# Attention denominators read over 128 partitions, and rows and down products in another order, in an adaLN block with linear attention and a GEGLU FFN

## The chip, the core and the metric

One core of a Trainium2 chip runs the whole block in one launch. The metric is device time in microseconds; three runs of the kernel before gave 782.70, 782.91 and 783.98, a median of 782.91. TensorE (PE) multiplies matrices out of weights loaded beforehand (PEld), VectorE (DVE) and ScalarE (ACT) work on rows, GpSimd (POOL) helps a little, and SyncE (SP) issues the DMAs, which 16 DMA engines carry out.

## What is computed

`x` is [1, 2048, 1024] bf16, with 32 heads of 32, `w_gate` and `w_up` [1024, 3584], `w_down` [3584, 1024], `c` [1, 1024], `w_mod` [1024, 6144]. Cut to what matters:

```
mod = silu(c) @ w_mod                       # six rows of 1024: sa ca ga sb cb gb
h   = layernorm(x) * (1 + ca) + sa
q, k, v = h @ wqkv                          # 32 heads
pq, pk  = phi(q), phi(k)                    # phi(t) = (t + 1 if t > 0 else exp(t)) + 1e-6
kv  = sum_s pk[s] v[s]^T ;  z = sum_s pk[s] # per head
o   = (pq @ kv) / (pq @ z + 1e-6)           # the divisor is "den"
x   = x + ga * (o @ wo)
h   = layernorm(x) * (1 + cb) + sb
out = x + gb * ((gelu(h @ w_gate) * (h @ w_up)) @ w_down)
```

## The kernel before

**Order of the work.** Every instruction is recorded with what it reads and writes; a tracker of intervals makes the waits. TensorE and SP run in the order in which the program records their instructions. The order of DVE, ACT and POOL between two marks (from the k projections to the loads of FFN unit 0) is made by a list scheduler from a table of costs and the due times of what depends on an instruction. All DMAs of the main part go through SP's one queue, in order; they take eight lanes (semaphores) in turn, and a DMA waits until the one before it in its lane is complete. The tokens are 16 chunks of 128, in four superblocks `sg` of four chunks.

**Until about 127 us** TensorE makes k and q (L880, L934), in bf16.

**127 to 191 us**: 24 m_tiles (L895) of 16 matmuls with 341 or 342 columns multiply the transposed pk with x. After each of them a table `HOOK` (L1302) puts in smaller work, by name: `kv<g>` is kv_prod (L913), eight 128-column matmuls on a transposed m_tile that m_t (`mT<g>`, L703, a transposing DMA into `mtb`) has brought; `w<i>` is w2_pair (L1201, copied out at L1208), which folds kv and wo into `W2`; `modp` is mod_pass (L1227), which sums modulation rows over partitions with mod_rows (L840), copies them out (L847), stores 4 rows of 512 f32 to DRAM (L849) and loads them as columns `sbT`, `cbT` (L1230); `gbr` is gb_rows (L809), the same for gb from `HLG`, which gb_hilo (L801; its last DVE subtraction is called mlo7) writes; `den<i>` is the divisor of two superblocks (L1240).

```
HOOK = {0: "ga", 6: "kv0", 10: "kv1", 11: "w0", 13: "kv2", 15: "modp kv3 z32", 16: "den0", 17: "w1 rb0.0 rb0.1", 18: "",
        19: "kv4", 20: "den1 ps0.0", 21: "gbr", 22: "ps0.1", 23: "rb2.0"}
```

**1/den.** den adds 1e-6 (L1245), takes the reciprocal (L1246) and stores 128 rows of 256 f32 in DRAM (L1248) as `scr_rd[sg, h, k, g, t]`: h one of two halves of 256 tokens, k one of four heads within a group, g one of eight groups. In `PQ[sg]`, partition 32k + d holds component d of head k of each group. rb_load (L1260) brings 1/den into `RB`, with each of the four rows k copied to 32 partitions: per half four DMAs, one for each k. pq_scale (L1273) multiplies pq by it on DVE, four instructions of two groups for each half, each after all four DMAs of its half.

**191 to 257 us**: the wo stage (L1283), in chunks c0 to c15 of 16 matmuls with 512 columns; chunk c needs PQ of its half (c0, c1: half 0 of superblock 0, and so on). On DVE x1 (L1291) adds a chunk to x, then come the second layernorm and T2, a transposing DMA (`h2a`, `h2b`). A table `SLOT` (L1769) says what is recorded after each chunk: the other pq_scales, rb3, loads of x, and `wt_dma(0)` (L1371), FFN unit 0's weights, after chunk 4.

**241 to 600 us**: 28 units of the FFN's first half (L1458), each a 2 x 2 block product in seven products (Strassen's scheme in Winograd's form), with sums on DVE and ACT.

**598 to 776.6 us**: the down stage in eight pairs of chunks, again seven products (L1672) of up to 14 matmuls each. P1 and P2 take y and `w_down` in bf16, P5, P6, P7, P3, P4 sums in fp32 (`sb` by L1643 and L1648). d_pair (L1722) runs them in the order 1, 5, 6, 2, 7, 3, 4; P7 goes on in P6's bank; copies (L1692, L1698) and adds (L1695) join the banks, evac (L1576, L1577) scales by gb and adds x. The rows of y for the next pair (`ya`) come back from DRAM by y_in (L1571), x by x_in (L1568). Hooks for each pair (L1885) place these. Pair 0 is mixed with plain products (L1593). The tail is the last evac and its DMA.

Of the kernel before, what the change touches and what calls it, by code (L numbers as in the profile page):

```python
# [330 lines left out]
def bass_adaLN_cond__linear_attn_block__geglu_ffn__prompt_kernel(  # L331
# [18 lines left out]
    with ExitStack() as es:  # L350
# [183 lines left out]
        def r_2k(off, name):  # L534
            return [(off, off + 2048, name)]
# [256 lines left out]
        def gb_acc(j, dc):  # L792
# [4 lines left out]
            else:  # L797
                sch.op(V, lambda e: e.scalar_tensor_tensor(acc[:, :], src, SILF[:, dc:dc + 1], acc[:, :], op0=ALU.mult, op1=ALU.add),
                       rd=rs_ + rng, wr=rng, note=f"macc{6 + j}.{dc}")

        def gb_hilo(j):  # L801
            acc, rng = GA_[j]
            sch.op(A, lambda e: e.activation(HLG[:, j, 0, :], acc[:, :], ACTF.Copy), rd=rng, wr=r_hlg(j, 0), note=f"mhi{6 + j}")
            sch.op(V, lambda e: e.tensor_tensor(HLG[:, j, 1, :], acc[:, :], HLG[:, j, 0, :], ALU.subtract), rd=rng + r_hlg(j, 0), wr=r_hlg(j, 1), note=f"mlo{6 + j}")

        o_gb = [None]

        def gb_rows():
            mod_rows(((0, 2, 5, lambda j, h: (HLG[:, j, h, :], r_hlg(j, h))),))  # L809
            o_gb[0] = mod_store(2, 5, MRG, [(OFF_TMP + 4096, OFF_TMP + 5120, "mrg")], 2)  # L810

# [380 lines left out]
        def z32():  # L1192
            sch.op(V, lambda e: e.tensor_tensor(Z32[:], BM32[:], ZCOLS[:, :].unsqueeze(2).to_broadcast([P, NG, NH]), ALU.mult),
                   rd=r_sm("bm32") + r_sm("zcols"), wr=r_sm("z32"), note="z32")

        def w2_pair(i, b0=4):
            for hf in range(2):
                for r in range(2):
                    for h in range(2):
                        b, g = b0 + 2 * r + hf, 2 * i + h  # L1200
                        sch.op(T, lambda e, b=b, g=g, h=h, r=r, hf=hf: e.matmul(ps_all[64 * h:64 * h + 64, b * 512:(b + 1) * 512], KVT[64 * r:64 * r + 64, g, 0:64],  # L1201
                               WO[64 * r:64 * r + 64, g, hf * 512:(hf + 1) * 512], start=True, stop=True),
                               rd=r_kvt(g, g + 1) + r_wo(g, hf * 512, (hf + 1) * 512), pwr=pr(b), note=f"w2 {i}.{hf}", overwrite_ok=True)
            for r in range(2):
                b, g = b0 + 2 * r, 2 * i + r
                w_, p_ = W2[:, g, :], ps_all[:, b * 512:(b + 2) * 512]
                eng = V if i > 1 and r else A
                sch.op(eng, lambda e, w_=w_, p_=p_, eng=eng: e.activation(w_, p_, ACTF.Copy) if eng == A else e.tensor_copy(w_, p_),  # L1208
                       prd=pr(b) + pr(b + 1), wr=r_w(OFF_WK, "w2", g), note=f"w2cp{g}")
# [15 lines left out]
        def mod_pass():  # L1225
            assert mdone[0] >= 48 and not late
            mod_rows(((2, 4, 5, hl_src),))  # L1227
            o_r = mod_store(4, 5, MROW[1], r_2k(OFF_ROW + 2048, "mrow1"), 1)
            for dst, nt, a0 in ((SBT, "sbT", 0), (CBT, "cbT", 2)):
                sch.dma(Q, lambda e, dst=dst, a0=a0: e.dma_start(dst[:, :], scr_row[1, a0:a0 + 2, :].rearrange("a (b p) -> p (a b)", p=P)),  # L1230
                        wr=r_sm(nt), deps=[o_r], note=nt)

# [19 lines left out]
        o_rd = {}  # L1252
        rb_ops = {}

        def rb_load(sg, hs=(0, 1)):
            i = sg % 2
            for h in hs:
                made = []
                for k in range(HPG):
                    made.append(sch.dma(Q, lambda e, h=h, k=k: e.dma_start(  # L1260
                        RB[i][32 * k:32 * (k + 1), h, :, :].rearrange("p a b -> p (a b)"),
                        scr_rd[sg, h, k:k + 1, :, :].rearrange("k g t -> k (g t)").to_broadcast([32, NG * HW])),
                        wr=r_rb(i, h) if k == 0 else (), deps=made[0].deps if k else [o_rd[sg // 2]], note=f"rb{sg}.{h}.{k}"))
                rb_ops[sg, h] = made

        GH = [((0, 2), (2, 4)), ((4, 6), (6, 8))]

        def pq_scale(sg, h, gs):
            i, t0 = sg % 2, h * HW
            for g0, g1 in gs:  # L1270
                ap = PQ[sg][:, g0:g1, t0:t0 + HW]
                rng = r_pq(sg, g0, g1, t0, t0 + HW)
                sch.op(V, lambda e, ap=ap, i=i, h=h, g0=g0, g1=g1: e.tensor_tensor(ap, ap, RB[i][:, h, g0:g1, :], ALU.mult),  # L1273
                       rd=rng + r_rb(i, h, g0, g1), wr=rng, deps=rb_ops[sg, h], note=f"pqs{sg}.{h}.{g0}")

        x1_ops, s_ops = {}, {}

        def wo_mm(c_, b0, gs):
# [9 lines left out]
            if gs[-1] == NG - 1:  # L1288
# [12 lines left out]
        tiles = [(g, k) for g in range(4) for k in range(3)] + [(g, 0) for g in range(4, NG)] + [(g, k) for g in range(4, NG) for k in (1, 2)]  # L1301
        HOOK = {0: "ga", 6: "kv0", 10: "kv1", 11: "w0", 13: "kv2", 15: "modp kv3 z32", 16: "den0", 17: "w1 rb0.0 rb0.1", 18: "",  # L1302
                19: "kv4", 20: "den1 ps0.0", 21: "gbr", 22: "ps0.1", 23: "rb2.0"}
        st = {}

        def hook_run(f):
# [7 lines left out]
            elif f == "modp":  # L1314
                mod_pass()
            elif f == "z32":
                z32()
            elif f[:3] == "den":
                st[int(f[3:])] = den(int(f[3:]), 5)
                st[int(f[3:])]()  # L1320
# [7 lines left out]
        for n, (g, k) in enumerate(tiles):  # L1328
# [19 lines left out]
            for f in HOOK.get(n, "").split():  # L1348
                hook_run(f)
        wo_mm(0, 0, [0, 1, 2, 3])  # L1350
        w2_pair(2)
# [4 lines left out]
        rb_load(1)  # L1356
        rb_load(2, (1,))
        w2_pair(3)
        wo_mm(1, 2, [3, 4, 5])
# [8 lines left out]
        def wt_dma(u):  # L1368
            i, f0 = u % 2, u % NFP * 256
            for t, v_ in enumerate((wg_v, wu_v)):  # L1370
                sch.dma(Q, lambda e, t=t, v_=v_: e.dma_start(WT[i][:, t, :, :], v_[:, :, f0:f0 + 256]), wr=r_wt(i, t, t + 1), note=f"wt{t} u{u}")  # L1371

# [282 lines left out]
        def d_prod(ca, b0, k, own=None, js=None):  # L1655
            b = b0 + {1: 0, 2: 0, 5: 3, 6: 2, 7: 2, 4: 2, 3: 1}[k] if own is None else own
            i = {1: None, 2: None, 5: 0, 6: 1, 7: 2, 3: 3, 4: 4}[k]
            o = None
            js = range(nj(ca)) if js is None else js
            for j in js:  # L1660
# [5 lines left out]
                else:  # L1666
# [3 lines left out]
                    if i == 4:  # L1670
                        dst = dst.rearrange("p (h c) -> p h c", h=2)
                o = sch.op(T, lambda e, l_=l_, r_=r_, j=j, dst=dst: e.matmul(dst, l_[:, 0, :], r_, start=(k in (1, 5) or own is not None) and j == js[0], stop=j == js[-1], skip_group_check=True),  # L1672
                           rd=rl + rr, pwr=(pr(b) if j == js[0] else ()), note=f"down P{k} c{ca} j{j}", overwrite_ok=True)
# [30 lines left out]
        def d_pair0(hook):  # L1704
            parts = parts_of(0)
            for k in (2, 6, 5, 0, 7, 3, 13, 11, 12, 4):
# [13 lines left out]
                hook(k)  # L1720

        def d_pair(i, hook):  # L1722
            ca, b0 = 2 * i, i % 2 * 4
# [6 lines left out]

            for k in (1, 5, 6, 2, 7, 3, 4):
                if last and k == 3:
                    d_prod(ca, b0, 3, None, range(6, NDJ))
                    evac_part(*parts[1])
                    continue
                d_prod(ca, b0, k)
                if k == 1:
                    d_cp(b0 + 2, b0, "dpcp")
                elif k == 5:
                    d_ecp(b0 + 3)  # L1740
                    d_s(ca, 2)
                elif k == 6:
                    d_add(b0 + 1, b0 + 2)
                    d_s(ca, 3)
                    y_next(0)
                elif k == 2:
                    evac(*parts[0])
                elif k == 7:
                    d_add(b0 + 3, b0 + 2)
                    d_s(ca, 4)  # L1750
                    y_next(1)
                    evac(*parts[3])
                elif k == 3:
# [12 lines left out]
        def cb1():  # L1766
# [3 lines left out]
                3: lambda: pq_scale(1, 1, GH[0] + GH[1]),  # L1770
                4: lambda: (cb1(), wt_dma(0)),
                5: lambda: (pq_scale(2, 1, GH[0] + GH[1]), rb_load(3, (0,))),
# [111 lines left out]
        def hooks(i):  # L1884
            def hook(k):  # L1885
                more = i + 1 < 2 * CPG
                if i == 1:
                    if k == 1:
                        d_t(2, 5)
                        d_t(2, 6)  # L1890
                    if k in (6, 2, 7):
                        d_t(4, {6: 4, 2: 5, 7: 6}[k])
                    if k in (6, 7):
                        n = 1 if k == 6 else 2
                        evac(*parts_of(0)[n])
                        x_in(1, n)
                else:
                    if k == 1:
                        x_in(i, 0, 3, 1)
                    elif k == 5:  # L1900
                        x_in(i, 2)
                    if not more and k in (5, 6):
                        for q in {5: (0, 1), 6: (2,)}[k]:
                            t_gb(q)
            return hook

        d_pair0(hook0)
        for i in range(1, 2 * CPG):
            d_pair(i, hooks(i))
# [75 lines left out]
```

## Time and profile before

| what | us |
|---|---|
| median of 3 runs | 782.91 |
| profiled span | 780.9 |
| PE busy | 770.2 (99%) |
| PEld busy | 496.2 (64%) |
| DVE busy | 645.9 (83%) |
| ACT busy | 374.6 (48%) |
| POOL busy | 47.5 (6%) |

The profile is of one execution, and its times count from the start of its span. What lies around the span makes up the rest of the 782.91. "Idle before" is the time that an engine stood still ahead of an instruction, with what released it. A stretch's line gives the busy time of each engine in it and, last, TensorE's granted clock (1.00 is full speed), the share of time that the DMA engines were busy and what they moved. A group of DMAs has its time on the issuing queue; landing is told apart.

### The profile page before, as it was taken

To read this page: it belongs to the slowest core of one execution; us is meant where nothing else is said; L and a number is where in the kernel's file an instruction comes from. 1 tells how busy PE (TensorE), PEld (TensorE's weight loads), DVE (VectorE), ACT (ScalarE), POOL (GpSimd) and SP (SyncE) were. 2 spreads that over 40 slices of the span, in tenths; PEclk is the share of its full clock that TensorE was granted. 3 is DMA by queue.
4 is the path that set the end of the run, shared out by engine and by line. 5 is a ranking of instruction groups with operands and counts; after the bars stand their busy time and mean duration, and the time that the engine had idled before them with its cause. 6 is when DMAs were issued, how large, how long until landed. Compare 5 with 4: busy or idle time off the path is not lost.

```text
span 780.9 us, 10753 instructions
## 1 busy us (share of the span) xinstructions
PE 770.2 (99%) x3825; PEld 496.2 (64%) x3883; DVE 645.9 (83%) x964; ACT 374.6 (48%) x629; POOL 47.5 (6%) x126
## 2 busy tenths in 40 slices
PE   8999999999999999999999999999999999999998
PEld 4444445666445667667676767667676576677766
DVE  6699988897899878787989888888989888676767
ACT  2497743242466487878755555555555211111111
POOL 2031300000321011100000000000000000000000
PEclk9999999999999999999999999999999999999999
DMA  9879749939999358867353865535356334443331
GB/s 284 256 167 252 158 91 215 255 80 196 203 287 231 82 138 212 230 175 215 99 145 108 250 211 172 148 96 161 97 147 221 111 127 139 144 141 114 126 125 60
DMA packets 196940, 130.22 MB, mean 167 GB/s; under 512 B 69516, under 2 KB 182420, under 8 KB 195864
## 3 DMA queue, kind: packets, MB, share of 16 engines
q1 hardware_dynamic: 196872, 129.55, 62.4%
q8 instruction: 30, 0.49, 0.3%
q14 instruction: 22, 0.18, 0.1%
q10 hardware_dynamic: 16, 0.00, 0.0%
HBM read 92.55 MB, written 23.35 MB: 148 GB/s over the span
## 4 chain that ended last, share of the span: by engine, by line
PE 95%; SPq 2%; DMA 1%; DVE 1%; issue 1%; ACT 0%; DVEq 0%; ACTq 0%
PE ps_all L1458 45%; PE ps_all L1672 21%; PE ps_all L895 7%; PE ps_all L934 7%; PE ps_all L1283 7%; PE ps_all L880 5%; PE ps_all L1593 1%; SPq L598 1%; DMA wmq<-in_w_mod_dram 1%; SPq L603 1%; DMA h1T<-xh 0%; PE ps_all L913 0%; PE ps_all L1201 0%; PE ps_all L1240 0%; DVE h1T L724 0%
## 5 line engine op out<-in xcount | busy, mean ns | idle before, releaser
L1458 PE MATMUL ps_all<-ss,tp 128*128 128x512 f32 x896 | 214.3, 396 | 0.0
L1458 PEld LDWEIGHTS ps_all<-ss,tp 128*128 128x128 f32 x896 | 168.3, 188 | 37.8 <-DVE ss L1413 0.2
L1672 PE MATMUL ps_all<-dt,sb 128*128 128x512 f32 x424 | 102.5, 398 | 0.0
L1481 ACT ACTIVATE ge<-ps_all 128x512 f32<-128x512 f32 x112 | 64.1, 597 | 73.8 <-DVE ps_all L1469 62.1
L1458 PE MATMUL ps_all<-h2a,wt 128*128 128x512 bf16 x421 | 95.7, 379 | 1.8
L1672 PEld LDWEIGHTS ps_all<-dt,sb 128*128 128x128 f32 x424 | 79.6, 188 | 18.5 <-DVE sb L1648 0.3
L1476 DVE TENSOR_TENSOR ps_all<-ps_all,es 128x512 f32<-128x512 f32 x54 | 37.6, 699 | 49.4 <-ACT es L1466 49.0
L1488 DVE TENSOR_TENSOR ys<-ge,ps_all 128x512 bf16<-128x512 f32 x112 | 74.4, 684 | 3.8 <-PE ps_all L1672 0.5
L1458 PEld LDWEIGHTS ps_all<-h2a,wt 128*128 128x128 bf16 x448 | 38.0, 98 | 57.3 <-ACT ps_all L1463 16.9
L1433 DVE TENSOR_TENSOR tp<-wt 128x1024 fp32r<-128x1024 bf16 x56 | 68.1, 1217 | 1.8 <-DMA wt<-in_B_w_up_dram 1.8
L1433 DVE TENSOR_TENSOR tp<-wt,tp 128x1024 fp32r<-128x1024 bf16 x56 | 68.2, 1218 | 0.0
L934 PE MATMUL ps_all<-h1T,wq 128*128 128x512 bf16 x256 | 56.7, 379 | 0.0
L880 PE MATMUL ps_all<-wk,h1T 128*128 128x512 bf16 x239 | 55.3, 379 | 1.1 <-DMA wk<-in_A_wqkv_dram 0.5
L1283 PE MATMUL ps_all<-w,pq 128*128 128x512 bf16 x249 | 55.7, 379 | 0.5 <-issue 0.2
L1458 PE MATMUL ps_all<-ar,tp 128*128 128x512 f32 x224 | 55.5, 390 | 0.0
L869 ACT ACTIVATE eb<-ps_all 128x512 f32<-128x512 f32 x64 | 36.3, 594 | 37.6 <-PE ps_all L880 16.0
L1672 PE MATMUL ps_all<-wd,ya 128*128 128x512 bf16 x199 | 47.5, 380 | 0.7
L1458 PEld LDWEIGHTS ps_all<-ar,tp 128*128 128x128 f32 x224 | 42.1, 188 | 8.9
L1463 ACT ACTIVATE ps_all<-ps_all 128x512 f32<-128x512 f32 x56 | 32.6, 582 | 26.8 <-PE ps_all L1458 26.5
L934 PEld LDWEIGHTS ps_all<-h1T,wq 128*128 128x128 bf16 x256 | 25.0, 98 | 30.0
L1283 PEld LDWEIGHTS ps_all<-w,pq 128*128 128x128 bf16 x256 | 24.6, 98 | 30.3 <-issue 1.1
L1643 ACT ACTIVATE sb<-ya 128x896 fp32r<-128x896 bf16 (+1 forms) x16 | 14.5, 913 | 58.8 <-PE ps_all L1672 58.8
(141 smaller groups left out, 976.3 us busy)
## 6 DMA issues: line engine op xcount, KB each, us to landing
wt<-in_B_w_gate_dram SPq DMA_DIRECT2D x28, 512.0 KB, 4.0
wt<-in_B_w_up_dram SPq DMA_DIRECT2D x28, 512.0 KB, 5.2
scr_y<-ys SPq DMA_DIRECT2D x28, 512.0 KB, 3.2
ya<-scr_y SPq DMA_DIRECT2D x14, 896.0 KB, 4.9
rb<-scr_rd SPq DMA_DIRECT2D x32, 256.0 KB, 6.0
wd<-in_B_w_down_dram SPq DMA_DIRECT2D x7, 1024.0 KB, 7.6
wmst<-in_w_mod_dram SPq DMA_DIRECT2D x6, 1024.0 KB, 6.2
wmq<-in_w_mod_dram SPq DMA_DIRECT2D x8, 512.0 KB, 7.5
```

The source lines that it names most:

```text
L869: sch.op(A, lambda e: e.activation(EB[i][:, :], PS(bank), ACTF.Exp), prd=pr(bank), wr=rng, note=f"{note}.exp")
L880: o = sch.op(T, lambda e, dc=dc: e.matmul(PS(bank), H1[sg][:, ci, dc, :], W_[:, dc, jg * 512:(jg + 1) * 512], start=(dc == 0), stop=(dc == ...
L895: o = sch.op(T, lambda e, c_=c_: e.matmul(PS(bank, 0, n), PK[c_][:, g * P:(g + 1) * P], xrow(c_, o_, o_ + n), start=(c_ == 0), stop=(c_ == ...
L934: o = sch.op(T, lambda e, dc=dc: e.matmul(PS(b), WQ[:, dc, qc * P:(qc + 1) * P], H1[sg][:, :, dc, :], start=(dc == 0), stop=(dc == NDC - 1 ...
L1283: last[half] = sch.op(T, lambda e, g=g, half=half: e.matmul(PS(b0 + half), PQ[sg][:, g, ci * P:(ci + 1) * P], W2[:, g, half * 512:(half + ...
L1433: sch.op(V, lambda e: e.tensor_tensor(TP[k][:], in0, in1 if k in (0, 2) else in1[:], ALU.subtract), rd=r0 + r1, wr=r_tp(k), deps=[x1_ops[7 ...
L1458: o = sch.op(T, lambda e, l_=l_, r_=r_, dc=dc: e.matmul(PS(b), l_, r_, start=fresh and dc == 0, stop=dc == ND2 - 1, skip_group_check=True) ...
L1463: sch.op(A, lambda e: e.activation(PS(BB + t), PS(BA + t), ACTF.Copy), prd=pr(BA + t), pwr=pr(BB + t), note="pcp")
L1476: sch.op(V, lambda e: e.tensor_tensor(PS(BC + t), PS(BC + t), ES[t][:, :], ALU.add), prd=pr(BC + t), rd=r_2k(OFF_ES[t], f"es{t}"), pwr=pr( ...
L1481: sch.op(A, lambda e: e.activation(GE[i][:, :], PS(b), ACTF.Gelu_apprx_tanh), prd=pr(b), wr=r_2k(OFF_GE[i], f"ge{i}"), note="gelu")
L1488: sch.op(V, lambda e: e.tensor_tensor(YS[s_][:, 2 * h:2 * h + 2, t, :], q(GE[i][:, :]), q(PS(b + 1)), ALU.mult), rd=r_2k(OFF_GE[i], f"ge{i ...
L1672: o = sch.op(T, lambda e, l_=l_, r_=r_, j=j, dst=dst: e.matmul(dst, l_[:, 0, :], r_, start=(k in (1, 5) or own is not None) and j == js[0] ...
```

## The change

1. rb_load: still four DMAs for each half, each now with two of the eight groups for all 128 partitions, rows of 2 KB. The source is the four rows k, each read 32 times; k is the outermost dimension. Each pq_scale waits for its own DMA only. Three pq_scales are ordered behind other DVE work by added dependencies (the copy w2cp7, the subtraction mlo7).
2. The modulation rows of modp stand right ahead of den0 and w2_pair(1) right behind it; gbr stands right behind den1; the banks change with that. The loads of sbT and cbT go from behind modp to SP's place between mT6 and mT7.
3. wt_dma(0) moves from chunk 4 of the wo stage to right behind the rb loads that precede the wo chunks.
4. Down pairs run 5, 6, 7, 2, then P1 of the next pair, 3, 4. P7 starts a bank of its own in pairs 1 to 6 and is added by d_join (one more copy and one more add). The reads of y and x move along.

On SP the order becomes: modulation store, den0's store, mT4, rb0 (eight), mT5, den1's store, gb's store, mT6, sbT, cbT, mT7, rb2.0 (four), rb1 (eight), rb2.1 (four), unit 0's weights (two), T2 and x, rb3.0, T2 and x, rb3.1.

```diff
-            mod_rows(((0, 2, 5, lambda j, h: (HLG[:, j, h, :], r_hlg(j, h))),))
+            mod_rows(((0, 2, 6, lambda j, h: (HLG[:, j, h, :], r_hlg(j, h))),))
...
-            mod_rows(((2, 4, 5, hl_src),))
-            o_r = mod_store(4, 5, MROW[1], r_2k(OFF_ROW + 2048, "mrow1"), 1)
+            mod_rows(((2, 4, 2, hl_src),))
+            o_sc[0] = mod_store(4, 2, MROW[1], r_2k(OFF_ROW + 2048, "mrow1"), 1)
+        def mod_load():
             for dst, nt, a0 in ((SBT, "sbT", 0), (CBT, "cbT", 2)):
...
             for h in hs:
-                made = []
-                for k in range(HPG):
-                    made.append(sch.dma(Q, lambda e, h=h, k=k: e.dma_start(
-                        RB[i][32 * k:32 * (k + 1), h, :, :].rearrange("p a b -> p (a b)"),
-                        scr_rd[sg, h, k:k + 1, :, :].rearrange("k g t -> k (g t)").to_broadcast([32, NG * HW])),
-                        wr=r_rb(i, h) if k == 0 else (), deps=made[0].deps if k else [o_rd[sg // 2]], note=f"rb{sg}.{h}.{k}"))
-                rb_ops[sg, h] = made
+                for g0 in range(0, NG, 2):
+                    src = scr_rd[sg, h, :, g0:g0 + 2, :].rearrange("k g t -> k (g t)").unsqueeze(1).to_broadcast([HPG, P // HPG, 2 * HW])
+                    sch.dma(Q, lambda e, h=h, g0=g0, src=src: e.dma_start(
+                        RB[i][:, h, g0:g0 + 2, :].rearrange("p a b -> p (a b)"), src),
+                        wr=r_rb(i, h, g0, g0 + 2), deps=[o_rd[sg // 2]], note=f"rb{sg}.{h}.{g0}")
...
-                       rd=rng + r_rb(i, h, g0, g1), wr=rng, deps=rb_ops[sg, h], note=f"pqs{sg}.{h}.{g0}")
+                       rd=rng + r_rb(i, h, g0, g1), wr=rng, deps={(2, 0, 0): [w2_ops.get(7)], (2, 0, 2): [w2_ops.get(7)], (0, 0, 2): [mlo7[0]]}.get((sg, h, g0), []), note=f"pqs{sg}.{h}.{g0}")
...
-        HOOK = {0: "ga", 6: "kv0", 10: "kv1", 11: "w0", 13: "kv2", 15: "modp kv3 z32", 16: "den0", 17: "w1 rb0.0 rb0.1", 18: "",
-                19: "kv4", 20: "den1 ps0.0", 21: "gbr", 22: "ps0.1", 23: "rb2.0"}
+        HOOK = {0: "ga", 6: "kv0", 10: "kv1", 11: "w0", 13: "kv2", 15: "kv3 z32", 16: "modp den0 w1", 17: "rb0.0 rb0.1", 18: "",
+                19: "kv4", 20: "den1 gbr ps0.0", 22: "sbl ps0.1", 23: "rb2.0"}
...
-                st[int(f[3:])] = den(int(f[3:]), 5)
+                st[int(f[3:])] = den(int(f[3:]), (3, 5)[int(f[3:])])
...
         rb_load(1)
         rb_load(2, (1,))
+        wt_dma(0)
         w2_pair(3)
...
-            b = b0 + {1: 0, 2: 0, 5: 3, 6: 2, 7: 2, 4: 2, 3: 1}[k] if own is None else own
+            b = b0 + {1: 0, 2: 0, 5: 3, 6: 2, 7: 3 if 0 < ca < 4 * CPG - 2 else 2, 4: 2, 3: 1}[k] if own is None else own
...
+        def d_join(b0):
+            d_ecp(b0 + 3)
+            d_add(b0 + 3, b0 + 1)
+            d_add(b0 + 2, b0 + 2)
+
+        def d_open(i):
+            b = i % 2 * 4
+            d_prod(2 * i, b, 1)
+            d_cp(b + 2, b, "dpcp")
...
-            for k in (1, 5, 6, 2, 7, 3, 4):
+            for k in ((5, 6, 2, 7, 3, 4) if last else (5, 6, 7, 2, 1, 3, 4)):
...
+                if k == 1:
+                    d_open(i + 1)
+                    hook(k)
+                    continue
...
+                elif k == 7:
+                    if last:
+                        d_add(b0 + 3, b0 + 2)
+                    else:
+                        d_join(b0)
+                    d_s(ca, 4)
+                    evac(*parts[3])
                 elif k == 2:
+                    y_next(1)
                     evac(*parts[0])
...
-                4: lambda: (cb1(), wt_dma(0)),
+                4: lambda: cb1(),
...
         d_pair0(hook0)
+        d_open(1)
+        d_t(2, 5)
+        d_t(2, 6)
```

More of the change, by code (lines that the diff above doesn't have):

```diff
@@ L799, in gb_acc @@
                        rd=rs_ + rng, wr=rng, note=f"macc{6 + j}.{dc}")
+        mlo7 = [None]
         def gb_hilo(j):
@@ L803, in gb_hilo @@
             sch.op(A, lambda e: e.activation(HLG[:, j, 0, :], acc[:, :], ACTF.Copy), rd=rng, wr=r_hlg(j, 0), note=f"mhi{6 + j}")
-            sch.op(V, lambda e: e.tensor_tensor(HLG[:, j, 1, :], acc[:, :], HLG[:, j, 0, :], ALU.subtract), rd=rng + r_hlg(j, 0), wr=r_hlg(j, 1), note=f"mlo{6 + j}")
+            mlo7[0] = sch.op(V, lambda e: e.tensor_tensor(HLG[:, j, 1, :], acc[:, :], HLG[:, j, 0, :], ALU.subtract), rd=rng + r_hlg(j, 0), wr=r_hlg(j, 1), note=f"mlo{6 + j}")
         o_gb = [None]
         def gb_rows():
-            mod_rows(((0, 2, 5, lambda j, h: (HLG[:, j, h, :], r_hlg(j, h))),))
-            o_gb[0] = mod_store(2, 5, MRG, [(OFF_TMP + 4096, OFF_TMP + 5120, "mrg")], 2)
+            mod_rows(((0, 2, 6, lambda j, h: (HLG[:, j, h, :], r_hlg(j, h))),))
+            o_gb[0] = mod_store(2, 6, MRG, [(OFF_TMP + 4096, OFF_TMP + 5120, "mrg")], 2)
         def mod_acc(k, dc):
@@ L1194, in z32 @@
                    rd=r_sm("bm32") + r_sm("zcols"), wr=r_sm("z32"), note="z32")
+        w2_ops = {}
         def w2_pair(i, b0=4):
@@ L1207, in w2_pair @@
                 eng = V if i > 1 and r else A
-                sch.op(eng, lambda e, w_=w_, p_=p_, eng=eng: e.activation(w_, p_, ACTF.Copy) if eng == A else e.tensor_copy(w_, p_),
+                w2_ops[g] = sch.op(eng, lambda e, w_=w_, p_=p_, eng=eng: e.activation(w_, p_, ACTF.Copy) if eng == A else e.tensor_copy(w_, p_),
                        prd=pr(b) + pr(b + 1), wr=r_w(OFF_WK, "w2", g), note=f"w2cp{g}")
@@ L1226, in mod_pass @@
             assert mdone[0] >= 48 and not late
-            mod_rows(((2, 4, 5, hl_src),))
-            o_r = mod_store(4, 5, MROW[1], r_2k(OFF_ROW + 2048, "mrow1"), 1)
+            mod_rows(((2, 4, 2, hl_src),))
+            o_sc[0] = mod_store(4, 2, MROW[1], r_2k(OFF_ROW + 2048, "mrow1"), 1)
+        o_sc = [None]
+        def mod_load():
             for dst, nt, a0 in ((SBT, "sbT", 0), (CBT, "cbT", 2)):
                 sch.dma(Q, lambda e, dst=dst, a0=a0: e.dma_start(dst[:, :], scr_row[1, a0:a0 + 2, :].rearrange("a (b p) -> p (a b)", p=P)),
-                        wr=r_sm(nt), deps=[o_r], note=nt)
+                        wr=r_sm(nt), deps=[o_sc[0]], note=nt)
         HW = SGW // 2
@@ L1252, in bass_adaLN_cond__linear_attn_block__geglu_ffn__prompt_kernel @@
         o_rd = {}
-        rb_ops = {}
         def rb_load(sg, hs=(0, 1)):
@@ L1315, in hook_run @@
                 mod_pass()
+            elif f == "sbl":
+                mod_load()
             elif f == "z32":
@@ L1349, in bass_adaLN_cond__linear_attn_block__geglu_ffn__prompt_kernel, with wt_dma @@
                 hook_run(f)
+        def wt_dma(u):
+            i, f0 = u % 2, u % NFP * 256
+            for t, v_ in enumerate((wg_v, wu_v)):
+                sch.dma(Q, lambda e, t=t, v_=v_: e.dma_start(WT[i][:, t, :, :], v_[:, :, f0:f0 + 256]), wr=r_wt(i, t, t + 1), note=f"wt{t} u{u}")
         wo_mm(0, 0, [0, 1, 2, 3])
@@ L1366, in wd_dma @@
             sch.dma(Q, lambda e: e.dma_start(WDT[q][:], wd_v[:, f0:f1, :]), wr=[t_ for fc in range(f0, f1) for t_ in r_wd(fc)], note=f"wd{q}")
[L1368 to L1371, printed above, removed]
         def wo_chunk(c_, b0):
@@ L1671, in d_prod @@
                         dst = dst.rearrange("p (h c) -> p h c", h=2)
-                o = sch.op(T, lambda e, l_=l_, r_=r_, j=j, dst=dst: e.matmul(dst, l_[:, 0, :], r_, start=(k in (1, 5) or own is not None) and j == js[0], stop=j == js[-1], skip_group_check=True),
+                o = sch.op(T, lambda e, l_=l_, r_=r_, j=j, dst=dst: e.matmul(dst, l_[:, 0, :], r_, start=(k in (1, 5) or k == 7 and 0 < ca < 4 * CPG - 2 or own is not None) and j == js[0], stop=j == js[-1], skip_group_check=True),
                            rd=rl + rr, pwr=(pr(b) if j == js[0] else ()), note=f"down P{k} c{ca} j{j}", overwrite_ok=True)
@@ L1735, in d_pair @@
                     continue
+                if k == 1:
+                    d_open(i + 1)
+                    hook(k)
+                    continue
                 d_prod(ca, b0, k)
-                if k == 1:
-                    d_cp(b0 + 2, b0, "dpcp")
-                elif k == 5:
+                if k == 5:
                     d_ecp(b0 + 3)
@@ L1745, in d_pair @@
                     y_next(0)
+                elif k == 7:
[5 more added lines that the diff above has]
+                    evac(*parts[3])
                 elif k == 2:
+                    y_next(1)
                     evac(*parts[0])
[L1748 to L1752, printed above, removed]
                 elif k == 3:
@@ L1887, in hook @@
                 if i == 1:
[L1888 to L1893, printed above, removed]
+                    if k in (6, 2):
                         n = 1 if k == 6 else 2
@@ L1896, in hook @@
                         x_in(1, n)
-                else:
[L1898 to L1901, printed above, removed]
+                    if k in (6, 7, 2):
+                        d_t(4, {6: 4, 7: 5, 2: 6}[k])
+                else:
+                    if k == 5:
+                        x_in(i, 1, 2)
                     if not more and k in (5, 6):
@@ L1904, in hook @@
                             t_gb(q)
+                if more and k in (1, 4):
+                    x_in(i + 1, 3 if k == 1 else 0)
             return hook
         d_pair0(hook0)
+        d_open(1)
+        d_t(2, 5)
+        d_t(2, 6)
         for i in range(1, 2 * CPG):
```

## The prediction

> **What bounds the kernel now.** I read the chain that ended last first, then TensorE's waits, then the stretches around the edited code, then the DMA packets there.
>
> ```profile
> PE 95%; SPq 2%; DMA 1%; DVE 1%; issue 1%; ACT 0%; DVEq 0%; ACTq 0%
> ```
> ```profile
> PE ps_all L628 <- POOL bmask L581: 2.2, 1, 2.2
> PE ps_all L766 <- DMA wmq<-in_w_mod_dram: 1.0, 2, 0.6
> PE ps_all L880 <- DMA wk<-in_A_wqkv_dram: 0.5, 1, 0.5
> PE ps_all L880 <- DVE h1T L724: 0.2, 1, 0.2
> PE ps_all L1283 <- issue: 0.2, 1, 0.2
> ```
>
> TensorE is the bound: 95% of the chain, and its waits in all are 4.1 us of a span of 780.9, none of them on a DMA behind the start. So no wait is there to be removed around the edits; only TensorE's own time can shrink, and any new wait is added in full. Next, the table of stretches (PE, PEld, DVE, ACT, POOL busy, clock, DMA share, GB/s):
>
> ```profile
> 180.00:191.00 11.00, 11.00 (x111) 7.19 (x110) 8.03 (x14) 2.76 (x6) 0.00 (x0) 1.00 1.08 197
> 191.00:220.00 29.00, 28.68 (x154) 13.10 (x156) 23.17 (x45) 13.72 (x19) 9.73 (x22) 1.00 1.02 216
> 220.00:256.00 36.00, 35.84 (x164) 17.84 (x165) 33.22 (x54) 21.46 (x34) 5.66 (x13) 1.00 0.98 238
> ```
>
> PE is full, the clock is 1.00, and the DMA engines are full as well, at only 197 to 238 GB/s. That is where the 1/den loads run, and where the change works. The loads and their users:
>
> ```profile
> L1260 SPq DMA_DIRECT2D rb<-scr_rd x32: 302/419/1351, 176.7 to 236.4; - x32
> L1273 DVE TENSOR_TENSOR pq<-pq,rb x32: 628/684/693, 185.6 to 247.7; 128x512 bf16<-128x512 bf16 x32
>   DMA rb<-scr_rd: 2.2, 2
> ```
>
> DVE waited for them twice, 2.2 us, which TensorE did not feel. TensorE's order from there (start, us, engine, line):
>
> ```profile
> 190.42 0.61 PE L913 MATMUL ps_all<-mtb,wv 128*128 128x128 bf16 x8
> 194.57 1.05 PE L913 MATMUL ps_all<-mtb,wv 128*128 128x128 bf16 x16
> 197.21 44.41 PE L1283 MATMUL ps_all<-w,pq 128*128 128x512 bf16 x201 [0.16 <-issue]
> 248.58 3.63 PE L1283 MATMUL ps_all<-w,pq 128*128 128x512 bf16 x15
> ```
>
> kv_prod(5) at 190.42 needs the transpose mT5, which lies right behind the first eight rb loads in SP's queue: it landed at 189.58, with 0.84 us to spare. The wo chunks take 3.46 us each, so c4 starts at about 207.1, c6 at 214.0, c12 at 234.5; c14 stands at 248.58.
>
> **The 1/den loads.** Removed: per half of a superblock four loads of 32 rows of 8 KB. Added: four loads of 128 rows of 2 KB; 256 KB each, as before, and 32 in all, as before. An old load is 32 packets, two on each of 16 engines, of about 600 ns by the packets' records: 1.2 us, which is how the landings follow one another (180.26, 181.50, 182.67). A new one is 128 packets; 2 KB packets of x and of row stores took 84 to 89 ns. What counts is over how many engines the 128 are spread. A new load's destination has 128 rows, but its source runs over k outermost: 4 rows, each repeated 32 times. Two rows of the trace bear on it. The first is 200 to 210 us, with little but rb loads; the second 170 to 172.5 us, where the 4-row store of a modulation row ends beside one weight load:
>
> ```profile
> DMA packets 398, 2.20 MB, mean 220 GB/s; under 512 B 129, under 2 KB 129, under 8 KB 129
> ```
> ```profile
> DMA packets 482, 0.48 MB, mean 191 GB/s; under 512 B 20, under 2 KB 478, under 8 KB 482
> ```
>
> In the first, some 268 packets of 8 KB are 8.4 loads, beside 129 small ones (4 B, completions): about 16 a load, one for each engine. In the second, the four packets of 2 KB are the store; of the 20 small ones 16 are the weight load's, which leaves 4: a transfer whose outermost extent is 4 ran on 4 engines. No transfer of before has 4 on one side and 128 on the other, so I bound: on 16 engines 8 packets each, 8 x 84 = 0.67 us a load; on 4 engines 32 each, 32 x 84 = 2.69 us (89 ns: 2.85). I take 2.69: if both sides must be cut into equal parts, 4 is the most they share, and the 4-row store is the nearest row.
> [...]
>
> Now the queue, in order, at 2.69 us a load. Transfers start at 179.06 (first landing less 1.2). **rb0**: 8 loads to 200.6; rb0.0 is there at 189.8, in time for c0. **mT5** behind it lands at 201.6 (1 us, as before): kv_prod(5) is late by **11.2**. rden1's store, mrg, mT6, the two mod loads and mT7 follow, small, but each with a share on the four engines: about 4.4 us (mT6 and mT7 landed 0.9 and 2.2 behind the transfer ahead of them; 1.3 for the rest, an estimate), to 205.0. The mod loads, moved from 172 to between mT6 and mT7, cost no more than that share: their first reader, the add on cbT (L1767), came at 213.1. kv_prod(6, 7), now due at 205.8, get theirs just in time. **rb2.0, rb1, rb2.1**: 16 loads from 205.0, in steps of four: 215.8, 226.5, 237.3, 248.0. Every pq_scale waits only for its own load, then takes 0.7. The last quarter of c4 (before 209.7, now 220.9) needs rb1.0 whole: 226.5 + 0.7 = 227.2, late by **6.3** more. The last quarter of c6 (before 216.6, now 234.1) needs rb1.1: 238.0, **3.9** more. rb2.0 and rb2.1 (c8, c10) are in time. Behind them wt0 (512 KB twice, 2.7 us together) and T2 transposes: to about 253.5. **rb3.0** then lands at 264.3; c12's last quarter (before 237.1, now 258.5) waits until 265.0: **6.5** more. rb3.1 lands at about 277, c14's last quarter is due at 251.2 + 27.9 = 279.1: nothing. Sum: 11.2 + 6.3 + 3.9 + 6.5 = **27.9 us**. Each nanosecond a packet is 0.9 us of this (28 loads x 32 packets), so 89 ns gives about 32; if the small transfers slip in between the packets, the 9.9 us of gaps (4.4 and 5.5) go, and it is 18.
>
> **Rows in den's stretches.** mod_rows, den0 and w2_pair(1) now stand together, and the gbr rows behind den1: TensorE changes between 128-wide m_tile work and these narrow forms twice less and once less. A change in cost 92 to 100 ns in the start-to-start times (236 against 144 ns), so 0.28 + 0.19 = 0.47 us. gbr may wait some 0.3 us for the last DVE subtraction before it (mlo7). Both come ahead of the 11.2 us wait, which swallows them: 0.
>
> **The first FFN weights**: 1 MB ahead of the T2 transposes. They landed at 223.8 and unit 0 needs them at 241.45, so nothing is gained; the first T2 transpose, issued at 209.87, goes behind 2.7 us of them and is wanted at 241.45 too. 0.
>
> **Down pairs.** P5, P6, P7, then P2 with the next pair's P1, then P3, P4: P1 and P2 are bf16, the others fp32, so six pairs have one bf16 run fewer. Fourteen bf16 and 28 fp32 matmuls take 9.434 us, 14 and 42 take 12.606; so 14 fp32 take 3.172 and the bf16 run 3.089, against 14 x 215.8 ns = 3.021: 0.068 a run, 6 x 0.068 = **-0.4**. P7 in a bank of its own adds a DVE add (0.70) and an ACT copy (0.6) a pair, under a pair's 22.04 us; DVE is busy 133.6 of the stage's 176.6. The cover is thin elsewhere: P1 of the next pair wants its rows of y 12.8 us into the pair, and by issue (6.4) plus landing (5.0 to 6.05) they are there at 11.4 to 12.45.
>
> **Sum**: 780.9 + 27.9 - 0.4 = 808.4; the median of the runs, 782.91, lies 2.0 above the profiled span, so 810.4, or **810 us**.
>
> **Rivals.**
> Hidden anyway, the case on the other side (0.20): the loads use 16 engines. A load takes 0.67 us instead of 1.2, all ends earlier, TensorE had no wait there to lose. It decides at (190.42 - 1 - 179.06) / 8 = 1.3 us a load: below it mT5 is in time. Then only the runs count: 780.9 - 0.47 - 0.4 + up to 0.3, and 2.0: 782.2. For it: the old loads, with 32 rows, and all loads of 128 rows have 16 completions. Against: the 4-row store.
> Down slip (0.06): loads hidden, but y's rows come 0.5 us late in each of six pairs: 782.2 + 3 = 785.2. For: 0.35 us of room. Against: 5.0 us landings are the common ones.
> The forecast has 0.74. About 0.2%, 1.6 us, is what a measurement of this kernel can tell from no change. Faster by more 0.05 (the hidden case with more from the runs than counted), within 0.15, slower 0.80. The forecast's own range is 800 (no gaps) to 818 (89 ns, longer gaps), 0.63 of all; to hold 8 in 10 the range must reach down through the other cases to 781.5.
>
> **What would show it.** Right: rb packets of 2 KB with 4 completions a load, landings 2.7 us apart, a TensorE wait of about 11 us at L915 for mtb, waits at the wo matmuls whose pq waits for rb, and an FFN that is as long as before. Wrong: 16 completions, 0.67 us steps, and PE gapless from 180 to 256. If P1 waits for ya in the down stage, the last step failed.

## The result and the profile after

The changed kernel takes 831.38 us (831.06 to 832.74, 5 runs) against 782.91 (782.31 to 783.98): ratio 1.062, interval 1.0607 to 1.0633. It is slower, as forecast, but by 48.5 us and not by 27.5; 831 lies outside the range. The profiled span is 829.4 against 780.9, so the traces hold the whole difference.

The chain that ended last, by engine and by line, is no longer TensorE's alone:

```profile
PE 82%; SPq 10%; DMA 5%; issue 1%; DVE 1%; DVEq 0%
PE ps_all L1466 42%; PE ps_all L1680 20%; PE ps_all L936 7%; PE ps_all L897 6%; PE ps_all L882 6%; SPq L1267 5%; SPq L703 2%; DMA rb<-scr_rd 2%; DMA mtb<-mb 1%; PE ps_all L1601 1%; DMA h2a<-xl 1%; SPq L598 1%; DMA wmq<-in_w_mod_dram 1%; SPq L1360 1%; SPq L603 1%
```

SP's queue has 10% of the chain, most of it in issuing the 1/den loads (L1267) and the transposes (L703). From 170 to 310 us alone, where nearly all of the loss arises, the chain is by line:

```profile
by line: SPq L1267 32.5%; SPq L703 12.2%; DMA rb<-scr_rd 10.4%; DMA mtb<-mb 8.5%; DMA h2a<-xl 6.8%; issue 5.7%; PE ps_all L897 5.1%; PE ps_all L1466 5.0%; SPq L1360 4.5%; PE ps_all L1288 2.8%; DVE ss L1421 1.7%; DVE h2a L724 1.2%; PE ps_all
```

SP's issues and the landings of what it issued are 75% of this stretch. TensorE's waits, which were 4.1 us in all, now begin with:

```profile
PE ps_all L1288 <- DVE pq L1278: 13.0, 9, 4.0
PE ps_all L915 <- DMA mtb<-mb: 10.6, 1, 10.6
PE ps_all L1288 <- DVE xall L1296: 6.6, 2, 5.7
PE ps_all L1466 <- ACT ps_all L1471: 2.6, 1, 2.6
PE ps_all L1466 <- DVE ss L1421: 2.6, 2, 2.4
PE ps_all L1466 <- DMA h2b<-xl: 2.2, 1, 2.2
```

The first two are the forecast ones: pq late for the wo chunks, the transpose late for kv_prod(5). The other four were not forecast. The DMA packets from 205 to 235 us, where nearly only the new loads run:

```profile
DMA  1222222222222222222222222223222222222222
DMA packets 1442, 2.89 MB, mean 96 GB/s; under 512 B 42, under 2 KB 42, under 8 KB 1440
```

The engines are busy for two tenths where they were full before. Some 1,400 packets of 2 KB are 10.9 loads, beside 42 small packets: about 4 completions a load, so 4 engines. A packet took no longer than was assumed: from 225 to 235 us, 496 of them kept the 16 engines 26.2% busy, 84 ns each. So a source row read 32 times is not slow in itself; too few engines are at work. The forecast mechanism is there.

What the forecast lacked shows in SP's own timeline (start, us that SP spent in issuing, line, DMA). Before:

```profile
217.80 0.57 SPq L1371 DMA_DIRECT2D wt<-in_B_w_gate_dram  x1
222.33 1.92 SPq L1260 DMA_DIRECT2D rb<-scr_rd  x4
224.35 1.23 SPq L703 DMA_TRANSPOSE h2b<-xl  x1
233.97 2.86 SPq L1260 DMA_DIRECT2D rb<-scr_rd  x4
```

After:

```profile
204.76 33.43 SPq L1267 DMA_DIRECT2D rb<-scr_rd  x14
238.24 2.43 SPq L1360 DMA_DIRECT2D wt<-in_B_w_gate_dram  x1
240.73 3.89 SPq L1360 DMA_DIRECT2D wt<-in_B_w_up_dram  x1
244.72 6.98 SPq L703 DMA_TRANSPOSE h2a<-xl  x1
258.29 2.35 SPq L1267 DMA_DIRECT2D rb<-scr_rd  x4
260.73 7.95 SPq L703 DMA_TRANSPOSE h2b<-xl  x1
278.62 2.62 SPq L1267 DMA_DIRECT2D rb<-scr_rd  x4
```

A load that took SP 0.4 to 0.5 us to issue takes 2.4 here on average (33.43 / 14): after the first four or five of a series SP stands still in each issue, mostly for about as long as one load takes on the four engines. That it waits there for room behind earlier loads is inferred from this pace alone (2.4 us an issue, 2.4 to 2.6 us a load): no view names what SP waits for. It isn't the wait for a lane: in the kernel before, that showed as a gap of 0.6 to 1.1 us ahead of an issue (from 197 us on), and here the gaps are 0.1 us at most. SP also stands at whatever follows: the first T2 transpose behind rb3.0 holds SP for 7.95 us, where it took 1.23. Rb3.1 is issued 20.3 us behind rb3.0, where it was 11.6.

### The profile page after: what moved, and what is told of

It reads as the page before. It is cut to its first block, busy times and chain, and to the rows that moved or that the text cites. A ratio compares the mean times of both kernels' runs of the same rounds, so it can differ in the third digit from the quotient of the medians.

```text
span 829.4 us, 10821 instructions
## 1 busy us (share of the span) xinstructions
PE 784.3 (95%) x3883; PEld 498.2 (60%) x3883; DVE 649.2 (78%) x970; ACT 376.4 (45%) x635; POOL 45.6 (6%) x126
## 4 chain that ended last, share of the span: by engine, by line
PE 82%; SPq 10%; DMA 5%; issue 1%; DVE 1%; DVEq 0%
PE ps_all L1466 42%; PE ps_all L1680 20%; PE ps_all L936 7%; PE ps_all L897 6%; PE ps_all L882 6%; SPq L1267 5%; SPq L703 2%; DMA rb<-scr_rd 2%; DMA mtb<-mb 1%; PE ps_all L1601 1%; DMA h2a<-xl 1%; SPq L598 1%; DMA wmq<-in_w_mod_dram 1%; SPq L1360 1%; SPq L603 1%
## 5 line engine op out<-in xcount | busy, mean ns | idle before, releaser
L1466 PE MATMUL ps_all<-h2a,wt 128*128 128x512 bf16 x448 | 101.7, 380 | 4.8 <-ACT ps_all L1471 2.6
L1288 PE MATMUL ps_all<-w,pq 128*128 128x512 bf16 x256 | 64.5, 407 | 19.8 <-DVE pq L1278 13.0
L1278 DVE TENSOR_TENSOR pq<-pq,rb 128x512 bf16<-128x512 bf16 x32 | 22.0, 692 | 41.6 <-DMA rb<-scr_rd 41.5
L1706 ACT ACTIVATE de<-ps_all 128x512 f32<-128x512 f32 x14 | 8.4, 597 | 90.3 <-PE ps_all L1680 90.3
```

The costliest lines, as they stand in the source:

```text
L1288: last[half] = sch.op(T, lambda e, g=g, half=half: e.matmul(PS(b0 + half), PQ[sg][:, g, ci * P:(ci + 1) * P], W2[:, g, half * 512:(half + ...
L1466: o = sch.op(T, lambda e, l_=l_, r_=r_, dc=dc: e.matmul(PS(b), l_, r_, start=fresh and dc == 0, stop=dc == ND2 - 1, skip_group_check=True) ...
```

## The experiments

The medians of before beside them were 782.6 to 783.2. "Late" below is the start of TensorE's first weight load of a wo chunk, less its start in the profile of before. Starts at c0 differ by up to 1 us between profiles for what happens before 127 us, so only differences of several us are read from them.

| kernel | us | ratio, interval | c1 late | c7 | c11 | c13 | c15 |
|---|---|---|---|---|---|---|---|
| the change | 831.38 | 1.062, 1.0607 to 1.0633 | 12.3 | 23.5 | 30.6 | 36.6 | 48.5 |
| e1 old loads | 784.85 | 1.0020, 1.0011 to 1.0028 | -0.1 | 0.3 | 0.3 | 0.3 | 1.9 |
| e2 new loads alone | 832.36 | 1.0632, 1.0617 to 1.0646 | 12.7 | 24.1 | 26.9 | 36.1 | 48.1 |
| e3 sixteen rows | 784.40 | 1.0019, 1.0011 to 1.0028 | 0.8 | 2.0 | 2.0 | 2.0 | 2.0 |
| e4 eight rows | 794.87 | 1.0158, 1.0142 to 1.0173 | 5.3 | 5.3 | 5.3 | 6.3 | 11.9 |
| e5 two waits filled | 830.51 | 1.0611, 1.0596 to 1.0625 | 11.8 | 30.8 | 31.9 | 37.7 | 48.7 |
| e6 superblock 3 only | 797.08 | 1.0180, 1.0165 to 1.0196 | -0.3 | 0.1 | 0.1 | 1.6 | 14.3 |
| e9 rb3 on ScalarE's queue | 841.03 | 1.0744, 1.0730 to 1.0759 | 12.6 | 33.0 | 52.0 | 54.7 | 58.3 |
| e13 superblocks 0 to 2 | 820.60 | 1.0482, 1.0466 to 1.0498 | 12.9 | 24.0 | 31.2 | 33.9 | 37.5 |
| e14 rb3.1 behind rb3.0 | 835.38 | 1.0670, 1.0652 to 1.0688 | 12.6 | 24.0 | 30.8 | 36.5 | 52.4 |
| e15 first wait filled | 831.71 | 1.0614, 1.0598 to 1.0630 | 11.5 | 24.2 | 31.4 | 37.1 | 48.5 |

**Is it the loads, and is it the number of engines?** Four kernels.

e1, the change with the old loads:

```diff
-                for g0 in range(0, NG, 2):
-                    src = scr_rd[sg, h, :, g0:g0 + 2, :]...to_broadcast([HPG, P // HPG, 2 * HW])
+                for k in range(HPG):
+                    made.append(...scr_rd[sg, h, k:k + 1, :, :]...to_broadcast([32, NG * HW]))
```

> The changed kernel with the old 1/den loads (four DMAs of 32 rows of 8 KB a half, each pq_scale after all four); everything else of the change stays. Theory A (the new loads run on 4 of the 16 DMA engines, 2.6 us each, and all of the loss of 48.5 us follows from that): the loss goes, 782.0 to 782.9, ratio to before 0.999 to 1.000. Theory B (half of the loss comes from the other moves, unit 0's weights and the modulation loads ahead of the T2 transposes): a loss of 10 us or more stays, 793 or above.

784.85 us: the loss comes from the loads, but for 1.6 us, which is more than theory A allowed and far less than theory B; e11 below finds where it comes from.

e2 is the same exchange the other way: before, with the new loads.

> The kernel before with the new 1/den loads only; the weights of unit 0 stay at chunk 4, rows and down pairs as before. Theory A: nearly the whole loss, 820 to 831; less than the changed kernel by what the 1 MB of weights ahead of the T2 transposes costs there (up to 8 us). Theory B: about 805, what the prediction's four waits alone gave.

832.36 us, all of it, and just above the expected 820 to 831. In the changed kernel, the early weights of unit 0 cost nothing on top: without them c11 is 26.9 late instead of 30.6, but c15 is nearly the same.

e3 and e4 store 1/den R times, so that the source has 4R rows outermost:

```diff
+                o_rd[pr_] = [sch.dma(Q, lambda e, r=r: e.dma_start(scr_rd[2 * pr_:2 * pr_ + 2, :, :, r].rearrange("s f k g t -> (s f k) g t"), RDC[:, :]),
+                                     rd=r_sm("rdc"), note=f"rden{pr_}.st") for r in range(R)]
...
+                    src = scr_rd[sg, h, :, :, g0:g0 + 2, :].rearrange("k r g t -> (k r) (g t)").unsqueeze(1).to_broadcast([HPG * R, P // HPG // R, 2 * HW])
```

> The changed kernel with 1/den stored four times in DRAM, so that the source of a new load has 16 different rows outermost, each read 8 times; still 128 rows of 2 KB. Four stores take the place of one behind each den. Theory A: 16 engines, 16 completions a load, 0.67 to 0.75 us a load, no wait of TensorE at kv_prod(5) or the wo chunks, 782 to 784. Rival C (what is slow is rows of 2 KB or a source read many times, not the number of engines): loads stay at 2 us or more, 815 or above.

> The same with two stores, so that the source has 8 different rows outermost, each read 16 times. Theory A: 8 engines, 8 completions a load, 16 packets each, 1.3 to 1.4 us a load: just over the 1.2 of before, TensorE waits at kv_prod(5) for 0 to 2 us, 782 to 787. Rival C: no different from 16 rows, or from 4.

784.40 (0.4 above its bracket) and 794.87 us. Rival C falls: rows are still 2 KB and the same bytes come in, and with 16 rows the loss is 1.5 us; that a row is read less often there does not explain it, since a packet took 84 ns even where it was read 32 times. Between 4, 8 and 16 rows the loss falls as the number of rows grows. The DMA packets of e4 (184 to 190 us) and of a kernel with 16 rows (e8, 200 to 212 us), where the loads run:

```profile
GB/s 193 259 329 352 265 207 218 191 205 205 191 205 205 218 191 218 205 191 205 205 205 205 205 218 177 218 191 205 218 191 218 191 205 205 205 205 205 205 219 177
```
```profile
DMA  6999989799999999899999999999999999999999
DMA packets 1856, 3.32 MB, mean 277 GB/s; under 512 B 200, under 2 KB 250, under 8 KB 1855
```

Eight rows move 205 GB/s, twice the 101 of four; sixteen move 277, not four times as much: the engines are full (9) and a load takes 0.95 us (262 KB at 277 GB/s) where 0.67 was expected. e4 missed its 782 to 787. At 205 GB/s a load takes 1.28 us, and I had counted a wait of 0 to 2 us at kv_prod(5) only; it waited 3.7 us, and c14 and c15 lost 5.5 more in the way the changed kernel does.

**Why 48 and not 27?**

e6 takes the new loads for superblock 3 alone, e13 for superblocks 0 to 2 (`if sg != 3` and `if sg == 3` call the old rb_load).

> The changed kernel with the old loads for superblocks 0 to 2 and the new ones for superblock 3 only. Ring theory (the sum of the prediction: a load costs its 2.6 us of the four engines and nothing else): rb3.0 transfers from 225 to 235.5, ahead of chunk 12's need at 237, rb3.1 by 249, no wait of more than 1 us; 784 to 786. Theory E (SP itself stands still while it issues a DMA for which the queue has no room, and the T2 transposes behind it come late with all that waits for them): T2 of chunk 4 is issued over 5 us late, unit 0 waits for h2b, 787 to 793.

> The changed kernel with the new loads for superblocks 0 to 2 and the old ones for superblock 3: the other half of the run with superblock 3 alone, which lost 14.5 us. Theory E (one serial queue: SP's issue and the engines behind it, so that the halves add up): 48.5 - 14.5 = 34 us lost, 814 to 820. The prediction's own terms up to chunk 6 (11.2 + 6.3 + 3.9 = 21.4): 803 to 806.

797.08 and 820.60 us: 14.5 and 37.7 lost, 52 together against 48.5. In e13 only 3.6 us are lost from c13 to c15, where the change loses 12: most of that last part comes with superblock 3's loads. Both are well above what the prediction's terms gave (about nothing and 21.4), and nearly add up; e6 lies above its bracket of 787 to 793, e13 just above 814 to 820. SP's timeline of e6:

```profile
226.05 7.75 SPq L703 DMA_TRANSPOSE h2b<-xl  x1
```

Four loads of 2.6 us are enough to hold the transpose behind them for 7.75 us; then TensorE waits in unit 0, and 2.9 us in all for pq. In unit 0:

```profile
245.20 1.89 PE L1482 MATMUL ps_all<-h2a,wt 128*128 128x512 bf16 x8 [2.17 <-DMA h2b<-xl]
249.75 3.39 PE L1482 MATMUL ps_all<-h2a,wt 128*128 128x512 bf16 x8 [2.66 <-ACT ps_all L1487]
264.65 3.78 PE L1482 MATMUL ps_all<-ss,tp 128*128 128x512 f32 x8 [2.43 <-DVE ss L1437]
```

e9 takes rb3 off SP's queue: `rb_load(3, (0,), A)` and `rb_load(3, (1,), A)` behind the pq_scales of superblock 1, with eight lanes for ScalarE.

> The changed kernel with the eight loads of superblock 3 on ScalarE's DMA queue, recorded behind the pq_scales that free their buffer, so that they don't stand behind T2 transposes on SP, nor these behind them. Theory E (SP's order and its standing still make the second half of the loss): rb3 lands before 275 instead of 272 to 295, the waits at unit 0 and chunks 12 to 15 shrink, 808 to 820. Rival (the second half comes from the T2 chain itself, through DVE and ScalarE): 825 or above.

841.03 us, worse: the expectation fell. From c13 to c15 only 3.6 us are lost instead of 12, as theory E has it, but c5 to c7 lose 12.9 instead of 3.4 and c7 to c11 19 instead of 7: the eight loads now share the four engines with rb1 and rb2.1. SP's issues of rb2.1 took 4.9 us each instead of 2.4, and the first T2 transpose was issued at 259.2 instead of 244.7. TensorE waited up to 10.0 us for x1 there. The loss moved.

e14 puts rb3.1 ahead of four T2 transposes (`rb_load(3)` in slot 5).

> The changed kernel with rb3.1's four loads right behind rb3.0's on SP, ahead of the T2 transposes of chunks 4 to 7, which then stand some 10 us longer. In the changed kernel rb3.1 was issued from 278.6 and was there at 295, and the chain ran through it. If rb3.1 alone sets the end: it is there at about 284, and the time falls by 8 to 10 us, 821 to 824. Theory E (SP's queue is the bound, and what is taken from one entry is given to the next): unit 0 waits for h2b instead, and the time is 829 to 834.

835.38 us: no gain, 4 lost, and above the 829 to 834 of theory E too. c14 then waits for nothing of pq, but unit 0 stands for 9.9 us:

```profile
289.16 3.57 PE L1466 MATMUL ps_all<-h2a,wt 128*128 128x512 bf16 x8 [9.87 <-DVE xall L1296]
```

DVE was late with that x1 because it had stood for 9.0 us until a load of x landed. SP issued this load at 279.6, behind rb3 and a T2 transpose that held it for 7.46 us. Theory E expected the wait at h2b; it came at another entry, but what one entry of SP's queue gains the next ones lose.

**Is TensorE's own slowness part of it?** Behind four of its waits in the changed kernel (10.6, 4.0, 5.7 and, before 299.3, 2.4 us) TensorE is slow for a while. Start, us, operation behind the first and the third:

```profile
201.96 3.06 PE L1288 MATMUL ps_all<-w,pq 128*128 128x512 bf16 x8
261.52 5.70 PE L1288 MATMUL ps_all<-w,pq 128*128 128x512 bf16 x16 [5.70 <-DVE xall L1296]
```

and the stretches around them (the clock is the third number from the end):

```profile
180.00:203.00 23.00, 11.87 (x110) 7.68 (x108) 9.70 (x16) 2.72 (x6) 0.00 (x0) 0.81 0.69 113
250.00:270.00 20.00, 12.54 (x47) 4.55 (x44) 12.08 (x28) 11.77 (x15) 6.40 (x14) 0.83 1.05 148
```

Single matmuls start 427 ns apart there instead of 216; 34 such intervals are 7 us. The granted clock was 0.50 from 201.2 to 204.3, 223.3 to 228.2, 261.5 to 265.7 and 300 to 303 us, and 1.00 right behind the first and the third: 3.2 us of slow work behind the wait of 10.6, 4.2 behind that of 5.7.

e15 fills the first wait with matmuls that nobody reads; e5 also put 15 ahead of c4:

```diff
+                fill(46)
                 kv_prod(5, 4)
...
+                if c_ == 4:
+                    fill(15)
                 wo_chunk(c_, 2 * (c_ % 4))
```

> The changed kernel with 46 matmuls that nobody reads ahead of kv_prod(5) only, in banks that nobody waits for. They keep TensorE busy for 9.9 of the 10.6 us of its wait. Clock term: the 5 matmuls of 427 ns behind the wait (1.05 us too long) run at 216, and chunk 0 is 1 us earlier against kv_prod(5). Whether the end moves tells if TensorE is the bound there: 830.4 if it is, 831.4 within 0.4 if SP's queue is.

> The changed kernel with matmuls whose result nobody reads in two of TensorE's waits: 46 ahead of kv_prod(5) (9.9 us of its 10.6) and 15 ahead of chunk 4 (3.2 us of about 5). In the changed kernel 512-column matmuls take 427 instead of 216 ns for 2 to 4 us behind each long wait; 5 behind the first, 10 behind the second. Theory D (a slow clock behind the waits is a term of its own, missing in the sum): those 15 run at 216 ns, and the time falls by 1 (the first wait alone) to 3 us, 828.4 to 830.4. Rival (the landings of the loads set the end whatever TensorE does between): no change, 831.4 within 0.5.

e15: 831.71 us. The slow matmuls are gone (c0 takes 1.67 us for seven, as before), c1 is 11.5 late instead of 12.3, and the end has not moved. In e5 the second filling did something else than was meant: its bank still held c3, whose x1 stands on DVE behind the late pq_scales:

```profile
PE ps_all L1305 <- DVE xall L1296: 12.8, 1, 12.8
```

So c4 was 30.8 late instead of 16.6. c15 was 48.7 late, as in the change, and the time 830.51, between the two brackets; its ratio's interval overlaps that of the change, so no gain is shown. Fourteen microseconds more of waiting at c4 cost nothing: TensorE is not the bound up to c11 (about 262 us), and its early waits are cover.

**The rest of the change.** e11 is e1 with unit 0's weights back behind chunk 4.

> The changed kernel with the old 1/den loads, and unit 0's weights back behind chunk 4. With the old loads and the early weights, 1.7 us were lost at chunks 14 and 15. If the early weights make that (the first T2 transpose stood 7 us in SP behind them), it goes: 782.0 to 782.8. Rival (the modulation loads, or pq_scale's order): 783.8 or above, the waits at chunks 14 and 15 stay.

782.82 us, ratio 0.9998 (0.9989 to 1.0007), against 784.85 and 1.0020 for e1: the early weights cost 1.7 us (0.0022 of 783) where the loads are the old ones. SP in e1, in front of the first T2 transpose, which took 1.23 before:

```profile
209.73 6.91 SPq L703 DMA_TRANSPOSE h2a<-xl  x1
```

e10 is before with the new order of the down pairs.

> The kernel before with the new order of the down pairs only. By the sum of the prediction six bf16 runs less give 0.4 us; by the traces of the kernels with 8 and 16 rows 0.2 to 0.3. So 782.2 to 782.7, no difference that can be told from noise. Rival (the next pair's rows of y come too late for P1): TensorE waits for ya in each of six pairs, 785 or above.

783.05 us, ratio 1.0000 (0.9992 to 1.0009). In its trace TensorE ends 0.07 late after being 0.41 late at c14, so what follows is 0.34 shorter, and no wait for ya is on its list.

**Toward a better version**: e8 is e3 with rb0.1 behind mT5 (`17: "rb0.0"`, `19: "kv4 rb0.1"`); e12 moves den0's stores behind mT4 and the modulation loads behind mT7 as well (`17: "st0 rb0.0"`, `23: "sbl rb2.0"`).

> Sixteen different source rows as before (four stores), with the four loads rb0.1 moved from ahead of mT5 to behind it on SP. With sixteen rows TensorE's only new wait was 2.0 us at kv_prod(5), for mT5. If that wait is SP issuing eight loads and six more stores ahead of it, it goes: 781.9 to 782.7, that is 0.5 to 1.3 below before. Rival (mT5 is late by the three added stores alone): the wait stays at 1 us or more, 783.4 or above.

> Sixteen source rows, with what made TensorE wait 2 us in that kernel moved: den0's four stores behind mT4, rb0.1 behind mT5, the modulation loads behind mT7. If those waits (1.2 at kv_prod(4), 1.0 to 1.6 at kv_prod(5) to (7)) are only the order in SP's queue, they go, the rows keep their 0.3 and the down pairs theirs: 782.0 to 782.6, 0.0 to 0.6 below before. Rival (the stores of 128 KB each load the engines): 783.5 or above.

784.72 (1.0027, 1.0017 to 1.0036) and 785.64 us (1.0037, 1.0024 to 1.0051): both missed. The expectation of e8 misread where e3 waits: not at kv_prod(5), but 1.2 us at kv_prod(4) and 1.0 at kv_prod(7). With rb0.1 behind mT5, e8 waits 1.2 and 1.6 us at the same two. e12 is rid of the wait at kv_prod(4) and waits 1.3 us at kv_prod(6) and 0.4 at kv_prod(7): the six more stores, about 0.6 us of SP each, come ahead of one or another of mT4 to mT7. In e12's profile TensorE ends only 1.2 us late; the other 1.7 us of its longer span lie in the landing of the last output DMA. No version beat the kernel before; e11 equals it.

## Why the prediction was right and wrong, step by step

By lateness in the changed kernel, the 48.5 us arise as 12.3 up to c1, 11.2 from c1 to c7, 7.1 to c11, 5.9 to c13 and 12.0 to c15. The prediction had 11.2, 10.2, 0, 6.5 and 0: nearly all of the miss lies in the two parts that it put at nothing.

- **Four engines, 32 packets each**: right. A load takes 2.4 to 2.6 us (101 GB/s) where 2.69 was taken. That both sides must be cut into equal parts was an assumption; the runs show 4 completions a load and, from 4, 8 and 16 source rows, 101, 205 and 277 GB/s.
- **kv_prod(5), 11.2**: right, 10.6. **c4, 6.3 and c6, 3.9**: 7.8 and 3.4 (lateness of c5 less c1, of c7 less c5), the first with ten slow matmuls in it.
- **c10 and c11, in time**: wrong. They lost 7.1 us, 5.7 in one wait for x1. DVE, in order, stood at the second layernorm of chunks whose T2 transposes came late (issued from 244.7, where 209.9 was before), and the x1 that c11 waits for is behind it. The profile names no releaser for the 6.04 us; that it was T2 is read from the inputs, of which cbT and sbT had been loaded long before, and in e2, with T2 issued from 238.9, c11's wait was 2.2 us:

```profile
258.18 2.14 DVE L724 TENSOR_SCALAR h2a<-h2a,cb1T,sbT 128x256 bf16<-128x256 bf16 x8 [6.04 <-issue]
260.23 1.22 DVE L1296 SCALAR_TENSOR_TENSOR xall<-ps_all,xall 128x1024 bf16<-128x1024 f32 x1
```

- **c12, 6.5**: 5.9 from c11 to c13, of which two are slow matmuls.
- **"rb3.1 lands at about 277 ... nothing"**: this is the step that failed. The last pq_scale of rb3.1 began at 295.1. I let loads, weights and T2 transposes follow one another on the engines and took 5.5 us for wt0 and T2 ahead of rb3.0 and 2 for those ahead of rb3.1. They are also in series on SP, which stands in its issues: from the last issue of rb2.1 at 235.8 to the first of rb3.0 22.5 us pass, from the first of rb3.0 to the first of rb3.1 20.3. Unit 0 and c14, c15 then lost 12 us (36.6 to 48.5) where nothing was counted.
- **"Any new wait is added in full"**: the sum of TensorE's waits was the wrong frame. It gave the right size only where nothing later set the end; e5 and e15 show that early waits fall away. Here the bound of 120 us was SP's queue, and the sum had to be made along it.
- **Rows**: 0.47 forecast. The m_tile stage is 0.32 shorter in e1 and e11 (first m_tile to last 60.44 against 60.76) and 0.29 longer in the changed kernel, where gbr waits 0.6 us for mlo7 instead of 0.3; either way it is swallowed there.
- **The first FFN weights, 0**: right in the changed kernel (e2 without them is no faster), wrong with the old loads, 1.7 us. I looked at when the weights are needed, not at what stands behind them on SP.
- **Down pairs, -0.4**: 0.34. Their cover held.
- **Hidden anyway**: refuted by the packets. With loads on 16 engines e3 took 784.4, not 782.2, but it has six stores more.

What stays open: how the 12 us at unit 0, c14 and c15 share between rb3.1 and what stands behind rb3.0 on SP, T2 and the loads of x. e9 and e14 moved one and lost at the other, so no share can be given to either alone.

## What to carry to other kernels

Before reshaping a DMA, write down the outermost extent of both its sides, and count completions in the trace: here 128 rows at the destination were no help where the source had four (4 completions a load, 101 GB/s). When a transfer gets slower on a queue that an engine shares with everything else, sum along that queue, issue times included, and not over the waits of the engine that was the bound before. A DMA moved ahead can cost what is queued behind it, as the early weights did with the old loads (1.7 us).

## What the runs showed of the hardware

- In the changed kernel SP issued the first four or five 256 KB loads of 4 engines in a series at 0.5 to 0.7 us each, then stood 2.4 to 2.8 us in most further ones (1.1 to 4.8 at the extremes). A transposing DMA behind such a series held SP for 7.4 and 8.0 us there, and for 7.0 behind the two weight loads that followed one; in the kernel before the ones at these three places took 1.23 each. Behind old loads, with 16 completions each, and 1 MB of weights one held it for 6.91 us (e1).
- Loads of 2 KB rows moved 101, 205 and 277 GB/s from 4, 8 and 16 source rows (256 KB in 2.6, 1.28 and 0.95 us); the loads of 8 KB rows to 32 partitions moved 218 (256 KB in 1.2 us).
